# Scores on 64x128 tiles, a widened scale that is transposed, one of two value products scaled by GpSimd, and new step orders in an attention and squared-ReLU kernel

## The chip, the cores and the metric

The kernel runs on one core of a Trainium2 chip. Its time is the device time of one execution in microseconds (us); before the change the median of three runs is 1318.46 us (1316.78 to 1321.82). Five engines work beside each other and wait for each other through semaphores: PE (matrix products and transposes; PEld are its weight loads), DVE (VectorE), ACT (ScalarE), POOL (GpSimd) and SP, which only issues transfers. PE writes to PSUM alone; GpSimd doesn't read PSUM. PSUM has eight banks of 512 float32 columns.

## The reference

Threshold attention over 8 batches, 8 heads, 576 positions and 64 channels, then a two-layer network with a squared ReLU on the 4608 x 512 result. The two weight matrices come as float64.

```python
scores = scale * np.matmul(q, k.transpose(0, 1, 3, 2))
thresh = np.max(scores, axis=-1, keepdims=True) - tau
scores = np.where(scores >= thresh, scores, -1000000000.0)
scores = scores - np.max(scores, axis=-1, keepdims=True)
attn = np.exp(scores)
attn = attn / (np.sum(attn, axis=-1, keepdims=True) + 1e-09)
attn_out = np.matmul(attn, v).astype(np.float32)
...
h = np.maximum(x @ w_in, 0.0)
return (h * h @ w_out).astype(np.float32)
```

## The kernel before

It has an attention stage (to about 519 us) and then the two layers, each as nine steps of 49 products of a twice nested seven-product scheme (L812 and L947). The sums of weight blocks that this scheme needs are made by GpSimd in the attention stage (L122 and L125, 128x512 each).

**Attention, by periods.** The 32 pairs of heads are cut into 144 units of 128 queries (two heads, j = 0 and 1); every ninth unit is made of the 64 rows left over from two pairs. A period takes two units, A and B. `period(p)` walks through a list of step names, written out by hand, and each step records its instructions at that place; so the list fixes the order on every engine's queue. The list CONVERTING serves the periods 2 to 34, in which also one block of float64 weights is turned to float32 (steps c1 to c6, by integer work on ACT, DVE and GpSimd); the list PLAIN serves the others. In plain periods from 35 on, s1 and s2 each issue one GpSimd sum of weight blocks (s2 up to period 59).

**The steps.** `SA` and `SB` are the scores of A and B on PE (L434): 64x64 array tiles, four at once (two heads by two halves of the queries), 512 keys and then the 64 that are left. `SA` holds the leftover keys of both units. `topA0` and the like (L452, DVE) copy a unit's scores from PSUM and take the row maximum; `least` (L459, GpSimd, two columns) adds the threshold; `pow` (L462, ACT) is the exponential; `mask` (L467, DVE, both inputs in SBUF) zeroes what is under the threshold and sums each row. `over` (L474, GpSimd) and `inv` (L477, DVE) make one over the sum. `V`, `W` and `U` turn the weights of finished units on PE (L379, half transposes of 64 rows, so 64*128 tiles), and `eV`, `eW`, `eU` (L523, ACT) bring the result to SBUF as wT. `W` also spreads one over the sum along columns: eight matmuls with the identity (L515, 64*64 tiles). `PV` (L532, 64*64 tiles) is the value product of the units of two periods ago, and `x` (L638, DVE) multiplies its two halves with the spread scales and issues the store of x and the load of new values. `T` and `eT` turn queries and keys of later pairs (L397 on PE; L402 and L410 on ACT) and issue the loads of further ones. `fetch` loads a weight block.

**PSUM.** Scores of A lie in banks 0, 1, 4 and 5, those of B in 1 to 4. `PV` reuses banks 0 and 5, so the next `SA` waits for `x`; `T` uses banks 1 and 4, `W` banks 2 and 3. `U` and `V` share one buffer in banks 6 and 7. The function `touch` adds the waits between instructions of different engines on one bank, which is why the first top waits for the last instruction of `SA`.

**Rings.** Raw weight blocks have four buffers, wT and x two each, values three.

Of the kernel before, what the change touches and what calls it, by code (L numbers as in the profile page):

```python
# [10 lines left out]
FP32 = mybir.dt.float32  # L11
I32 = mybir.dt.int32
U32 = mybir.dt.uint32
ALU = mybir.AluOpType
# [34 lines left out]
def kernel(  # L49
# [25 lines left out]
    nc = tc.nc  # L75
    B, H, S, D = q.shape
    P = 128
# [3 lines left out]
    FULL = S // P  # L81
# [115 lines left out]
    def pick(t, k):  # L197
        return t.rearrange("p (n two) -> p n two", two=2)[:, :, k]

    def convert1(m):  # L200
        if m not in raws:
            return
        lo, hi = pick(raws[m], 0), pick(raws[m], 1)
        a = cv.tile([P, WC], I32, tag="a", bufs=3, name="a")
        nc.scalar.activation(out=a.bitcast(FP32), in_=hi.bitcast(FP32), func=AF.Abs)
        parts[m] = (lo, hi, a)
        raws.pop(m)

    def convert2(m):
        if m in parts:  # L210
            lo = parts[m][0]
            nc.scalar.activation(out=lo, in_=lo.bitcast(U32), func=AF.Copy, bias=0.0, scale=2.0**-29)

    def convert3(m):
# [24 lines left out]
    def convert6(m):  # L239
        if m not in parts:  # L240
            return
        lo, hi, a = parts.pop(m)
        if m < 16:
            a = weight(m)[:, :].bitcast(I32)
        nc.gpsimd.tensor_tensor(out=a, in0=hi, in1=lo, op=ALU.add)
        if m >= 16:
            nc.sync.dma_start(out=slot_of(*chunks[m][1:3]), in_=a.bitcast(FP32))
# [142 lines left out]
    def turn(i, which, spots, other=None):  # L390

        nat, to = loaded.pop((i, which)), places(i)
        of = [nat[:, t, :] for t in range(FULL)] + ([loaded.pop((i, 2))] if which else [])
        for t, x in enumerate(of):
            for r, (spot, at) in enumerate(spots):
                rows = ds(r * HALF, HALF)
                made = nc.tensor.transpose(spot[:, ts(t, HALF)], x[rows, :], ident[rows, rows])  # L397
                touch("turns", made, at, BANK)
        half = FULL * HALF

        def scaled(to, spot):
            touch("turned", nc.scalar.activation(out=to, in_=spot[0], func=AF.Identity, scale=qscale[:, :]), spot[1], BANK, i)  # L402

        def then():
            part = lambda r, x, n: (spots[r][0][:, ds(x, n)], spots[r][1])
            if which:
                for r, n in ((0, half), (1, half + REST)):
                    spot = part(r, 0, n)
                    copy_by = other if r and other else nc.scalar.copy
                    touch("turned", copy_by(to[1][:, ds(r * half, n)], spot[0]), spot[1], BANK, i)  # L410
                scaled(to[2], part(0, half, REST))
                next_keys(i)
            else:
                for r in range(2):
                    scaled(to[0][:, ds(r * half, half)], part(r, 0, half))
                if i + 1 < len(pairs):
                    load_q(i + 1)

        return then
# [3 lines left out]
    def scores(n, rest):  # L423

        of, t = units[n]
        at_k, count = (MAIN, REST) if rest else (0, MAIN)
        for j in range(2):
            first = n % 2 != j
            to = (3 * j + 1) * BANK + first * (BANK - REST) if rest else (3 * j + 2 * first) * BANK
            for c in range(2):  # L430
                rows, at = ds(j * D, D), ds(c * HALF, HALF)
                qT, kT, qR = turned[of[c]]
                lhs = qT[rows, ds((c * FULL + t) * HALF, HALF)] if t < FULL else qR[rows, :]
                made = nc.tensor.matmul(  # L434
                    sc[at, ds(to, count)], lhs, kT[rows, ds(at_k, count)], start=True, stop=True
                )
                touch("scores", made, to, count, of[c])

    def softmax(n):

# [40 lines left out]
    def do(n, what, *args):  # L481
        if n in soft:
            soft[n][what](*args)

    wT = {}
# [13 lines left out]
    def fill(m, f, pt, at=None):  # L499

        first, count = FILLS[f]
        if m not in wT:
            wT[m] = sb.tile([P, (2 * CH + 2) * P], FP32, tag="wT", bufs=W_RING, name="wT")
        for i, (u, c) in enumerate(FIRST[first : first + count]):
            half_turn(pt, i, weights[2 * m + u][:, c, :, :].rearrange("p j d -> p (j d)"), at)
        if f == "W":
            rs = smalls.pop(m)
            for j in range(2):
                for r in range(2):
                    rows = ds(r * HALF, HALF)  # L510
                    for u in range(2):
                        one = rs[rows, 3, 2 * u + j : 2 * u + j + 1]
                        wide = bass.AP(tensor=one.tensor, offset=one.offset, ap=[one.ap[0], [0, D]])
                        to = pt[ds(u * D, D), r, ts(count + j, HALF)]
                        made = nc.tensor.matmul(to, wide, ident[rows, rows], start=True, stop=True)  # L515
                        touch("turns", made, at and at + r * BANK, BANK)

    def filled(m, f, pt, at=None):

# [69 lines left out]
    def begun(n):  # L589
        return starts.get(n)  # L590

    PLAIN = """
        SA c3 T topA0 over U eU s1 SB topA1 powA1 leastA topB0 powB0 c1 s2 PV c4 V fetch
        inv powA0 c5 topB1 powB1 eT maskA1 x W eV maskA0 leastB c2 c6 eW maskB0 maskB1
    """.split()
    CONVERTING = """
        fetch c3 SA c1 SB topA1 over s1 U topA0 c2 powA1 topB0 topB1 eU leastA maskA1
        leastB inv powA0 PV powB0 W maskA0 x powB1 maskB0 T c4 c5 maskB1 eT V c6 eW eV
    """.split()

    def spots():
# [5 lines left out]
    def period(p):  # L607
# [26 lines left out]
        def given_out():  # L634
            if has(2 * m):
                x = sb.tile([P, 2, P], FP32, tag="x", bufs=2, name="x")
                for j in range(2):
                    made = nc.vector.tensor_tensor(  # L638
                        out=x[:, j, :], in0=sc[:, ds(5 * j * BANK, P)], in1=wT[m][:, ts(SCALE_AT + j, P)], op=ALU.mult
                    )  # L640
                    touch("x", made, 5 * j * BANK, P, m)
                wT.pop(m)
                valued(m)
                give_x(m, x)
            ask(False)

# [12 lines left out]
        def every(key):  # L659
# [8 lines left out]
            "PV": PV, "x": given_out,  # L668
# [4 lines left out]
        }  # L673
        steps["over"] = lambda: do(a, "over")
        steps["inv"] = lambda: do(a, "inverse")
        for letter, n in (("A", A), ("B", B_)):
# [533 lines left out]
```

## Time and profile before

| what | us |
|---|---|
| median of three runs | 1318.46 |
| the runs | 1321.82, 1318.46, 1316.78 |
| span of the profiled execution, first to last instruction | 1314.0 |
| PE busy, share | 1277.6, 97% |
| DVE busy, share | 1016.3, 77% |
| ACT busy, share | 849.6, 65% |
| POOL busy, share | 839.0, 64% |
| last tops of the attention stage end near | 508 |
| first product of the layers | 519.4 |

The granted clock of TensorE is 0.998 over the span. What a run's time holds beyond the span lies around the first and the last instruction. In a group of the profile one reads line, engine, operation, destination and source, shapes and count, then the busy time in us, the mean of one in ns, and the engine's idle time ahead of the group with what ended it. In a timeline one reads start and length in us, engine, line and operation.

### The profile page before, as it was taken

To read this page: it belongs to the slowest core of one execution; us is meant where nothing else is said; L and a number is where in the kernel's file an instruction comes from. 1 tells how busy PE (TensorE), PEld (TensorE's weight loads), DVE (VectorE), ACT (ScalarE), POOL (GpSimd) and SP (SyncE) were. 2 spreads that over 40 slices of the span, in tenths; PEclk is the share of its full clock that TensorE was granted. 3 is DMA by queue.
4 is the path that set the end of the run, shared out by engine and by line. 5 is a ranking of instruction groups with operands and counts; after the bars stand their busy time and mean duration, and the time that the engine had idled before them with its cause. 6 is when DMAs were issued, how large, how long until landed. Compare 5 with 4: busy or idle time off the path is not lost.

```text
span 1314.0 us, 47792 instructions
## 1 busy us (share of the span) xinstructions
PE 1277.6 (97%) x19483; PEld 1141.4 (87%) x19483; DVE 1016.3 (77%) x2497; ACT 849.6 (65%) x1464; POOL 839.0 (64%) x958
## 2 busy tenths in 40 slices
PE   7999999899999999999999999999999999999998
PEld 5666666677777777999999999999999999999998
DVE  5999999999999996877887788777656654665463
ACT  5999999888989886566756675665524322432240
POOL 1444444455555421778987888758777777777775
PEclk9999999999999999999999999999999999999999
DMA  5555566544433322466656655669645135423411
GB/s 135 143 160 142 155 174 182 149 103 99 101 78 86 77 60 46 148 206 192 195 180 210 197 187 179 193 232 394 249 161 161 48 115 162 161 63 100 161 33 33
DMA packets 247035, 192.12 MB, mean 146 GB/s; under 512 B 97184, under 2 KB 195488, under 8 KB 246816
## 3 DMA queue, kind: packets, MB, share of 16 engines
q1 hardware_dynamic: 245360, 188.63, 47.4%
q8 instruction: 153, 2.51, 0.8%
q10 hardware_dynamic: 1456, 0.44, 0.1%
q14 instruction: 66, 0.54, 0.1%
HBM read 116.65 MB, written 72.35 MB: 144 GB/s over the span
## 4 chain that ended last, share of the span: by engine, by line
PE 85%; ACT 8%; DVE 3%; issue 2%; DMA 1%; SPq 1%; POOL 0%; ACTq 0%; DVEq 0%; POOLq 0%
PE ph L812 30%; PE po L947 28%; PE sc L434 9%; PE sc L532 8%; PE pt L379 5%; ACT arena L523 3%; ACT arena L462 3%; PE sc L397 2%; PE sc L515 2%; DVE arena L452 1%; PE sc L379 1%; DMA wall<-w 1%; ACT arena L402 1%; DVE arena L467 0%; DMA arena<-in_k_dram 0%
## 5 line engine op out<-in xcount | busy, mean ns | idle before, releaser
L125 POOL TENSOR_TENSOR arena<-arena 128x512 f32<-128x512 f32 (+1 forms) x314 | 378.0, 1222 | 134.5 <-DVE arena L125 120.5
L947 PE MATMUL po<-wall,arena 128*128 128x128 f32 x3528 | 395.0, 275 | 1.6 <-ACT arena L724 1.4
L947 PEld LDWEIGHTS po<-wall,arena 128*128 128x128 f32 x3528 | 394.3, 192 | 2.2 <-ACT arena L724 1.8
L812 PE MATMUL ph<-arena,wall 128*128 128x128 f32 x3528 | 394.2, 275 | 0.7 <-DVE arena L638 0.7
L812 PEld LDWEIGHTS ph<-arena,wall 128*128 128x128 f32 x3528 | 394.0, 192 | 0.8 <-issue 0.8
L125 DVE TENSOR_TENSOR arena<-ph,arena 128x512 f32<-128x512 f32 x378 | 256.4, 689 | 86.2 <-PE ph L812 66.0
L122 POOL TENSOR_TENSOR arena<-arena 128x128 f32<-128x128 f32 (+2 forms) x314 | 255.2, 814 | 48.6 <-DMA arena<-w 31.9
L125 DVE TENSOR_TENSOR arena<-po,arena 128x128 f32<-128x128 f32 x378 | 108.4, 290 | 167.6 <-PE po L947 163.4
L467 DVE SCALAR_TENSOR_TENSOR arena<-arena 128x576 f32<-128x576 f32 x288 | 229.6, 817 | 2.7 <-ACT arena L462 1.7
L462 ACT ACTIVATE arena<-arena 128x576 f32<-128x576 f32 x288 | 208.2, 778 | 14.1 <-DVE arena L452 7.0
L452 DVE TENSOR_SCALAR_CACHE_REDUCE arena<-sc 128x576 f32<-128x576 f32 x288 | 205.5, 751 | 13.3 <-ACT arena L523 5.5
L758 ACT COPY c<-arena 128x512 f32<-128x512 f32 (+1 forms) x303 | 173.5, 579 | 50.4 <-DVE arena L122 41.3
L532 PEld LDWEIGHTS sc<-arena 64*64 64x64 f32 x5760 | 154.0, 133 | 55.3 <-DVE arena L452 28.7
L532 PE MATMUL sc<-arena 64*64 64x128 f32 (+1 forms) x5760 | 176.7, 263 | 18.1 <-DVE arena L452 11.6
L122 DVE TENSOR_TENSOR arena<-arena,c 128x512 f32<-128x512 f32 (+1 forms) x267 | 174.9, 663 | 6.1 <-ACT c L758 4.0
L434 PE MATMUL sc<-arena 64*64 64x64 f32 (+1 forms) x2304 | 167.4, 414 | 5.6 <-ACT arena L402 5.6
L523 ACT COPY arena<-pt 128x1024 f32<-128x1024 f32 x144 | 146.6, 1018 | 24.8 <-PE pt L379 24.4
L724 ACT COPY arena<-po 128x128 f32<-128x128 f32 x63 | 16.6, 264 | 186.4 <-PE po L947 183.7
L459 POOL TENSOR_SCALAR arena<-arena,tau_p 128x2 f32<-128x2 f32 x144 | 75.1, 521 | 73.4 <-DVE arena L452 67.8
L724 ACT COPY arena<-ph 128x512 f32<-128x512 f32 x63 | 36.6, 581 | 124.2 <-PE ph L812 123.5
L379 PEld LDWEIGHTS pt<-ident,arena 64*128 64x128 f32 x2304 | 83.1, 139 | 38.2 <-ACT arena L523 25.6
L434 PEld LDWEIGHTS sc<-arena 64*64 64x64 f32 x2304 | 59.2, 134 | 52.2 <-ACT arena L402 26.4
(46 smaller groups left out, 896.1 us busy)
## 6 DMA issues: line engine op xcount, KB each, us to landing
g<-arena SPq DMA_DIRECT2D x144, 256.0 KB, 2.4
arena<-g SPq DMA_DIRECT2D x144, 256.0 KB, 4.4
w<-arena SPq DMA_DIRECT2D x60, 256.0 KB, 2.4
wall<-w SPq DMA_DIRECT2D x49, 256.0 KB, 5.2
arena<-w SPq DMA_DIRECT2D x44, 256.0 KB, 3.2
arena<-in_v_dram SPq DMA_DIRECT2D x32, 288.0 KB, 3.6
out_dram<-arena SPq DMA_DIRECT2D x70, 128.0 KB, 2.2
arena<-in_q_dram SPq DMA_DIRECT2D x64, 128.0 KB, 3.2
```

The costliest lines, as they stand in the source:

```text
L122: e.tensor_tensor(out=out, in0=x, in1=y, op=ALU.subtract)
L125: e.tensor_tensor(out=out, in0=x, in1=y, op=ALU.add)
L379: made = nc.tensor.transpose(pt[:, r, ts(slot, HALF)], of[rows, :], ident[rows, rows])
L434: made = nc.tensor.matmul(sc[at, ds(to, count)], lhs, kT[rows, ds(at_k, count)], start=True, stop=True)
L452: made = nc.vector.tensor_scalar(out=s[:, j, :], in0=sc[:, ds(at, S)], scalar1=1.0, scalar2=None, op0=ALU.mult, op1=ALU.min, accum_out=nmx ...
L462: nc.scalar.activation(out=w[:, :, j, :], in_=of(j), func=AF.Exp, bias=nmx[:, j : j + 1], scale=-1.0)
L467: nc.vector.scalar_tensor_tensor(out=w[:, :, j, :], in0=of(j), scalar=thr[:, j : j + 1], in1=w[:, :, j, :], op0=ALU.is_le, op1=ALU.mult, a ...
L523: touch("weights", nc.scalar.copy(joined(to), whole(pt, 0, count)), at, 2 * BANK, m)
L532: made = nc.tensor.matmul(sc[ds(u * D, D), ds(5 * j * BANK + row, count)], loaded_v[i][rows, (c - (u != j)) % CH, :], wT[m][rows, ds(weigh ...
L758: nc.scalar.copy(c, y)
L812: nc.tensor.matmul(to[:, j, :], W_IN[m, k][:, ts(j, P)], of[k][:, m - 1, :], start=(not more and j == 0), stop=True, skip_group_check=True,)
L947: nc.tensor.matmul(to, g[:, j, :], w[:, j, :], start=(not more and j == 0), stop=(j == 3), skip_group_check=True)
```

## The change

Five things are done.

1. The scores are made on 64x128 tiles: for a unit of one pair, one matmul per head over all 128 queries in place of two over 64. For that the transposed queries are stored in natural order. The leftover units keep 64x64 tiles.
2. One over the sum is spread by GpSimd: the step `spread` (function `widen`) copies the four columns to 128x256 in the part of wT that `W` will overwrite, and `W` turns this copy with four half transposes in place of the eight matmuls of L515.
3. Of the two halves of the value product, DVE scales the first as before; the second is copied from PSUM by ACT, and the new step `xs` multiplies it by its scales on GpSimd. `xs` also issues the stores.
4. Both lists of steps get a new order. In PLAIN, s2 now stands ahead of `over`, and `U` ahead of `SA`; in CONVERTING, `T` opens the period.
5. c2 may now run ahead of c1.

```diff
     def convert2(m):
-        if m in parts:
-            lo = parts[m][0]
+        if m in raws or m in parts:
+            lo = pick(raws[m], 0) if m in raws else parts[m][0]
...
             else:
+                blocks = to[0].rearrange("p (t r q) -> p r t q", r=2, q=HALF)
                 for r in range(2):
-                    scaled(to[0][:, ds(r * half, half)], part(r, 0, half))
+                    spot, at = part(r, 0, half)
+                    scaled(blocks[:, r, :, :], (spot.rearrange("p (t q) -> p t q", q=HALF), at))
...
-            for c in range(2):
-                rows, at = ds(j * D, D), ds(c * HALF, HALF)
-                qT, kT, qR = turned[of[c]]
-                lhs = qT[rows, ds((c * FULL + t) * HALF, HALF)] if t < FULL else qR[rows, :]
-                made = nc.tensor.matmul(
-                    sc[at, ds(to, count)], lhs, kT[rows, ds(at_k, count)], start=True, stop=True
-                )
-                touch("scores", made, to, count, of[c])
+            rows = ds(j * D, D)
+            if t < FULL:
+                qT, kT, _ = turned[of[0]]
+                parts = [(ds(0, P), qT[rows, ts(t, P)], kT, of[0])]
+            else:
+                parts = [(ds(c * HALF, HALF), turned[i][2][rows, :], turned[i][1], i) for c, i in enumerate(of)]
+            for at, lhs, kT, i in parts:
+                made = nc.tensor.matmul(sc[at, ds(to, count)], lhs, kT[rows, ds(at_k, count)], start=True, stop=True)
+                touch("scores", made, to, count, i)
...
         if f == "W":
-            rs = smalls.pop(m)
             for j in range(2):
-                for r in range(2):
-                    rows = ds(r * HALF, HALF)
-                    for u in range(2):
-                        one = rs[rows, 3, 2 * u + j : 2 * u + j + 1]
-                        wide = bass.AP(tensor=one.tensor, offset=one.offset, ap=[one.ap[0], [0, D]])
-                        to = pt[ds(u * D, D), r, ts(count + j, HALF)]
-                        made = nc.tensor.matmul(to, wide, ident[rows, rows], start=True, stop=True)
-                        touch("turns", made, at and at + r * BANK, BANK)
+                half_turn(pt, count + j, wT[m][:, ts(SCALE_AT + j, P)], at)
+
+    def widen(m):
+
+        if m not in wT:
+            wT[m] = sb.tile([P, (2 * CH + 2) * P], FP32, tag="wT", bufs=W_RING, name="wT")
+        one = smalls.pop(m)[:, 3, 0:1]
+        wide = bass.AP(tensor=one.tensor, offset=one.offset, ap=[one.ap[0], [1, 2], [2, 2], [0, D]])
+        to = wT[m][:, ds(SCALE_AT * P, 2 * P)].rearrange("p (j u d) -> p j u d", j=2, u=2)
+        nc.gpsimd.tensor_copy(out=to, in_=wide)
...
     PLAIN = """
-        SA c3 T topA0 over U eU s1 SB topA1 powA1 leastA topB0 powB0 c1 s2 PV c4 V fetch
-        inv powA0 c5 topB1 powB1 eT maskA1 x W eV maskA0 leastB c2 c6 eW maskB0 maskB1
+        fetch U s2 SA over SB topA0 eU topA1 powA0 leastA s1 topB0 V inv topB1 spread powA1 maskA1 eV powB0 leastB powB1 PV T maskA0 W x maskB1 eT maskB0 eW xs
     """.split()
     CONVERTING = """
-        fetch c3 SA c1 SB topA1 over s1 U topA0 c2 powA1 topB0 topB1 eU leastA maskA1
-        leastB inv powA0 PV powB0 W maskA0 x powB1 maskB0 T c4 c5 maskB1 eT V c6 eW eV
+        fetch T SA c3 topA1 SB over c2 U topA0 eU topB1 topB0 c4 inv powA1 powA0 leastA PV leastB powB0 eT maskA1 x maskA0 powB1 V maskB0 spread W c5 eW c6 eV xs maskB1 c1
     """.split()
...
+                by_vector = (0,)
                 for j in range(2):
-                    made = nc.vector.tensor_tensor(
-                        out=x[:, j, :], in0=sc[:, ds(5 * j * BANK, P)], in1=wT[m][:, ts(SCALE_AT + j, P)], op=ALU.mult
-                    )
+                    by = sc[:, ds(5 * j * BANK, P)], wT[m][:, ts(SCALE_AT + j, P)]
+                    if j in by_vector:
+                        made = nc.vector.tensor_tensor(out=x[:, j, :], in0=by[0], in1=by[1], op=ALU.mult)
+                    else:
+                        made = nc.scalar.copy(x[:, j, :], by[0])
                     touch("x", made, 5 * j * BANK, P, m)
+                late["x"] = x, [j for j in range(2) if j not in by_vector], wT[m]
                 wT.pop(m)
                 valued(m)
+
+        def scaled_x():
+            if has(2 * m):
+                x, js, by = late["x"]
...
+                for j in js if len(js) == 1 else ():
+                    nc.gpsimd.tensor_tensor(out=x[:, j, :], in0=x[:, j, :], in1=by[:, ts(SCALE_AT + j, P)], op=ALU.mult)
                 give_x(m, x)
             ask(False)
```

By queue, in a plain period of the changed kernel: PE has U, SA, SB, V, PV, T, W; DVE topA0, topA1, topB0, inv, topB1, maskA1, maskA0, x, maskB1, maskB0; ACT eU, powA0, powA1, eV, powB0, powB1, the copy of x, eT, eW; GpSimd s2, over, leastA, s1, spread, leastB, xs. In a converting period: PE has T, SA, SB, U, PV, V, W; DVE topA1, topA0, topB1, topB0, c4, inv, maskA1, x, maskA0, maskB0, c5, maskB1; ACT c2, eU, powA1, powA0, powB0, eT, the copy of x, powB1, eW, eV, c1; GpSimd c3, over, leastA, leastB, spread, c6, xs.

More of the change, by code (lines that the diff above doesn't have):

```diff
@@ L206, in convert1 @@
         parts[m] = (lo, hi, a)
-        raws.pop(m)
     def convert2(m):
-        if m in parts:
-            lo = parts[m][0]
+        if m in raws or m in parts:
+            lo = pick(raws[m], 0) if m in raws else parts[m][0]
             nc.scalar.activation(out=lo, in_=lo.bitcast(U32), func=AF.Copy, bias=0.0, scale=2.0**-29)
@@ L242, in convert6 @@
         lo, hi, a = parts.pop(m)
+        raws.pop(m)
         if m < 16:
@@ L636, in given_out @@
                 x = sb.tile([P, 2, P], FP32, tag="x", bufs=2, name="x")
+                by_vector = (0,)
                 for j in range(2):
-                    made = nc.vector.tensor_tensor(
-                        out=x[:, j, :], in0=sc[:, ds(5 * j * BANK, P)], in1=wT[m][:, ts(SCALE_AT + j, P)], op=ALU.mult
-                    )
+                    by = sc[:, ds(5 * j * BANK, P)], wT[m][:, ts(SCALE_AT + j, P)]
[3 more added lines that the diff above has]
+                        made = nc.scalar.copy(x[:, j, :], by[0])
                     touch("x", made, 5 * j * BANK, P, m)
+                late["x"] = x, [j for j in range(2) if j not in by_vector], wT[m]
                 wT.pop(m)
                 valued(m)
+        def scaled_x():
+            if has(2 * m):
+                x, js, by = late["x"]
+                if len(js) == 2:
+                    nc.gpsimd.tensor_tensor(
+                        out=x[:, :, :].rearrange("p j q -> p (j q)"), in0=x[:, :, :].rearrange("p j q -> p (j q)"),
+                        in1=by[:, ds(SCALE_AT * P, 2 * P)], op=ALU.mult,
+                    )
+                for j in js if len(js) == 1 else ():
+                    nc.gpsimd.tensor_tensor(out=x[:, j, :], in0=x[:, j, :], in1=by[:, ts(SCALE_AT + j, P)], op=ALU.mult)
                 give_x(m, x)
@@ L667, in period @@
             "SA": scored_a, "SB": scored_b,
-            "PV": PV, "x": given_out,
+            "PV": PV, "x": given_out, "xs": scaled_x,
             "c1": lambda: convert1(begun(p)), "c2": lambda: convert2(begun(p)),
@@ L673, in period @@
         }
+        steps["spread"] = lambda: has(2 * m + 2) and widen(m + 1)
         steps["over"] = lambda: do(a, "over")
```

## The prediction

> **What bounds the kernel now.** I read the table of windows first, to find the stages. Its columns are PE, PEld, DVE, ACT and POOL busy, then clock, DMA share, GB/s.
>
> ```profile
> 100.00:150.00 50.00, 46.34 (x1164) 31.83 (x1158) 49.37 (x144) 47.43 (x77) 22.08 (x33) 1.00 0.53 141
> ...
> 400.00:450.00 50.00, 49.35 (x1322) 37.35 (x1320) 47.99 (x145) 44.62 (x70) 25.73 (x37) 1.00 0.37 86
> ...
> 700.00:900.00 200.00, 200.00 (x1794) 200.00 (x1793) 155.48 (x244) 127.16 (x229) 154.76 (x179) 1.00 0.63 211
> ```
>
> Everything the change touches lies before 519 us. The two layers behind it keep PE busy without a gap and are untouched: 0 for them. In the converting periods (first row) DVE is busy 98.7%, ACT 95%. In the plain ones (second row) PE is the fullest and DVE has 96%. So no engine alone is the answer in the plain ones.
>
> From the timeline I took the start of every fourth L452 as the start of a period. The 33 converting periods (24.3 to 268.2 us) take 7.39 us on average, the quick ones 7.19. The 25 plain periods with two GpSimd sums each (to 433.4 us) take 6.61, the quick ones 6.44; eight with one sum 6.58; three with none 6.43.
>
> Then the groups, for durations (mean ns of one after the comma), here by form:
>
> ```profile
> L638 DVE TENSOR_TENSOR arena<-sc,arena 128x128 f32<-128x128 f32 x120 | 29.1, 285 | 0.2
> ...
> L219 POOL TENSOR_SCALAR arena<-arena 128x512 f32<-128x512 f32 x28 | 17.1, 611 | 0.0
> ...
> L474 POOL TENSOR_SCALAR arena<-arena 128x4 f32<-128x4 f32 x61 | 14.1, 232 | 85.7 <-DVE arena L467 83.3
> ...
> L122 POOL TENSOR_TENSOR arena<-arena 128x384 f32<-128x384 f32 x4 | 4.0, 1002 | 0.2
> ```
>
> What an instruction costs its engine is the distance to the next start, which the timeline gives: L452 (top) 0.68, L467 (mask) 0.74, L638 0.20, reciprocal 0.09, L227 0.46, L235 0.61 on DVE; L462 (power) 0.67, an eviction of 1024 columns 0.90, of 512 0.47 on ACT.
>
> PE, one plain period:
>
> ```profile
> 408.28 2.22 PEld L532 LDWEIGHTS sc<-arena 64*64 64x64 f32 x71 [0.28 <-issue]
> ...
> 410.67 0.57 PEld L379 LDWEIGHTS pt<-ident,arena 64*128 64x128 f32 x16 [0.17 <-issue]
> ...
> 411.16 0.20 PEld L379 LDWEIGHTS sc<-ident,arena 64*128 64x128 f32 x4
> ...
> 411.43 0.32 PEld L515 LDWEIGHTS sc<-ident,arena 64*64 64x64 f32 x16
> ```
>
> Each row is one step; 64*64 and 64*128 are the array tiles. Between neighbours with unlike tiles there is a hole: 0.17 us between the value product and the transposes, 0.07 before L515. By single starts, a change of tile costs 0.10 us, and the first pass behind it 0.05 more: 0.15. Four such changes stand in a plain period.
>
> Last the waits of GpSimd and masks on each other, from two timelines:
>
> ```profile
> 270.96 1.28 POOL L122 TENSOR_TENSOR wall<-wall 128x512 f32<-128x512 f32 x1
> 272.21 0.79 POOL L459 TENSOR_SCALAR arena<-arena,tau_p 128x2 f32<-128x2 f32 x1
> ```
>
> and, on DVE:
>
> ```profile
> 271.63 1.22 DVE L467 SCALAR_TENSOR_TENSOR arena<-arena 128x576 f32<-128x576 f32 x1
> 272.78 0.08 DVE L467 DVE_READ_ACCUMULATOR arena<-arena 128x1 f32 x1
> ```
>
> A mask (two inputs from SBUF) that finds a GpSimd sum running takes 1.22 instead of 0.81 us: it starts in earnest 0.19 us before the sum's end. The small L459 that waits behind this mask takes 0.79 instead of 0.29: it starts 0.68 after the mask did. The tops (one input from PSUM) and the sums don't disturb each other. So masks and GpSimd exclude each other.
>
> **The change, part by part.**
>
> 1. *Scores on 64x128 tiles.* Half the matmuls per period (16 fewer loads and 16 fewer passes), but the same streams: four quadrants ran at once, 0.431 us per 512-column pass, and two wide tiles need the same passes. Gain by themselves 0. The new order stands them next to transposes of the same tile, so two of four changes of tile go: 0.30 us. No row shows a wide matmul that isn't a transpose. Bounds: 0, if the two tiles run side by side as the half transposes do (a pair per 0.062 us); +0.43 per 512-column score step, if the second tile waits for the first one's second pass. I take 0: the quadrants do overtake each other so. The Trainium skill (TensorE: Matmul & The Clock Gate, LDWEIGHTS) has a load last by its columns, about 107 ns for 128 against 53 for 64; by it the 64-column passes would grow by an estimated 0.05 each, 0.2 a period. The trace disagrees: loads of 128 columns show 139 ns against 133, and pairs follow each other at 0.062.
> 2. *Spread.* 16 passes of L515 (four groups at 0.058 = 0.23 us) go, four transposes (two pairs, 0.12) come. PE's plain period: 6.16 us of work with the changes of tile, then 5.75.
> 3. *Widening copy on GpSimd, 128x256.* No row shows one. Between 0.23 (four columns, L474) and 0.61 (512 columns, L219); half way by columns 0.42.
> 4. *One of two L638.* DVE loses 0.20. ACT gets a copy of 128x128; the page has L724 with 0.264, its slot about 0.16. GpSimd gets a 128x128 product: 384 columns take 1.00, 512 take 1.28, so 0.45 (bounds 0.23 and 1.00).
> 5. *Orders.* DMA issues move with their steps on SP: the store of x now waits for GpSimd. x has two buffers and a landing takes 2 to 4 us, so this stays hidden; if it didn't, the next x would wait.
>
> *Converting periods.* DVE then has 4x0.68 + 0.46 + 0.09 + 4x0.74 + 0.20 + 0.61 = 7.03. ACT had 6.6 to 6.7 and gets 0.16; PE 5.75. On GpSimd, the copy comes when the first mask ends, 0.68 after its start; the vector product of 0.20 stands between that mask and the next, and covers the copy up to 0.45. The conversion's last add (L245, 1.2) waits for the last mask and runs under the tops. In the slower old periods the mask behind the reciprocal waited 0.10 to 0.16 for its power; in the new order each power ends before its mask's turn. So 7.03, with 0.05 for the periods with a rest unit: 7.08 against 7.39, times 33 = **-10.2 us**.
>
> *Plain periods with sums.* I lay one out from the first top, t = 0. DVE alone would need 6.16 - 0.20 = 5.96. Loop over ACT: powers at 0.80 and 1.48, eviction 2.15, powers 3.05 and 3.73, copy of x 4.40, done 4.66; then scores 1.09 and 0.25 to the next top: 6.0. PE: top at 1.5, 2.27 for values with the change of tile and release, T, W and U 1.05, scores 1.34: 6.1. All three have room under what GpSimd does to the masks. The first small step (L459) starts at 1.56, the sum behind it 1.82 to 3.10: mask 1 at 2.91 instead of 2.78. The copy runs 3.58 to 4.00: mask 2 at 3.81. The second L459 4.48 to 4.77: mask 3 at 4.83. The product comes when mask 3 ends, 5.50 to 5.95: mask 4 at 5.76, the end 6.50. With 0.07 for rest units 6.57 against 6.61: 25 x -0.04 = **-1.0**. One sum: the same, 8 x -0.01 = -0.1. No sum: only the product hurts, 6.20 against 6.43, **-0.7**. What DVE and PE are relieved of is given back to GpSimd.
>
> Sum -12.0. The profiled execution spans 1314.0 and would span 1302; the median of the runs is 1318.46, 4.5 above that span. Forecast **1306**, own range 1298 to 1313.
>
> **Rivals.**
>
> *A sum between two masks (slower).* The other sum of a period no longer waits for the last mask through L474: it stands right behind the product. In my layout the copy of x is done at 4.66, GpSimd can begin the product near 4.76, and mask 3 asks at 4.83. If the product is first, mask 3 moves to 5.02; the sum, waiting, gets its turn at 5.70, before mask 4 asks at 5.76; mask 4 then starts at 5.70 + 1.28 - 0.19 = 6.79, and the period is 7.53. That is 25 x 0.92 = +23, less 11 for the rest: **1330**. The order is decided by 0.07 us, less than I know the copy (it decides from 0.35 up), ACT's copy or a semaphore's way. For it: the central numbers. Against it: it needs both that the product wins, and that a waiting GpSimd instruction beats the next mask, which the trace shows only with a reciprocal between; and two further waits (for the store of the old x) stand ahead of the product on GpSimd's queue, where an instruction with a wait elsewhere starts 0.09 behind the one before it. The Trainium skill (SBUF — State Buffer, Who interferes with whom) says that the one that issues first holds the shared port for its whole instruction and the other fully blocks; that favours this rival, and the 1.22 us mask bears it out but for the last 0.19.
>
> *GpSimd starves.* If DVE keeps masks back to back, the copy waits for mask 2 and ends at 4.62; W, U and the scores follow, next top 6.77. 33 plain periods get 0.17 worse, +6 - 11: **1313**. No row shows it.
>
> *Wide tiles one after the other.* PE 5.75 + 0.86 = 6.6 in plain periods, hidden in the converting ones: +3 - 11, **1311**. Against it: the overtaking quadrants.
>
> **How the numbers follow.** Forecast 0.55 (0.50 of it faster by over 0.5%, which is 6.6 us and about what a measurement of this kernel tells from no change); the sum between masks 0.30, slower; the two others 0.15, of which 0.05 faster and 0.10 within. The range has to reach the slow rival: 1297 to 1332. Faster 0.55, same 0.15, slower 0.30.
>
> **What would show it.** Converting periods at 7.0 to 7.1 with L515 gone and holes on PE only around the value product. Plain periods at 6.5 with masks of 0.9 to 1.1 us; if one mask in four takes 1.8 us in the plain periods with two sums, the rival holds. Score steps of over 1.2 us per 512 columns prove the wide tiles wrong. Scale transposes waiting for GpSimd would show starving. The prediction is wrong if converting periods stay above 7.3: then DVE wasn't their bound.

## The result: slower, by a sum between two masks

The changed kernel takes **1334.69 us** (median of 4 runs, 1333.93 to 1334.93) against 1318.66 before on the same chip (4 runs, 1316.78 to 1321.82): ratio 1.0119, 95% interval 1.0102 to 1.0137. The forecast was 1306; the rival "a sum between two masks" had said 1330. The profiled execution spans 1333.1 us, at a mean clock of 0.996 (before: 1314.0 at 0.998), 19.1 us more. The medians differ by 16.0. Most executions on record take 1.8 us more than their span; so by my estimate the profiled execution of before took some 1315.8, less than any of the four timed ones, and some 3 us of the 19.1 come from that.

The table of windows of the changed kernel; columns PE, PEld, DVE, ACT and POOL busy, then clock, DMA share, GB/s:

```profile
100.00:150.00 50.00, 46.37 (x1012) 35.15 (x1010) 49.60 (x143) 49.72 (x88) 31.27 (x51) 1.00 0.56 143
400.00:450.00 50.00, 45.92 (x976) 33.73 (x972) 50.00 (x121) 39.89 (x69) 37.04 (x48) 1.00 0.31 69
```

In the plain periods (second row) PE fell from 49.35 to 45.92 and ACT from 44.62 to 39.89, while POOL rose from 25.73 to 37.04 and DVE shows no idle time at all, in a kernel in which DVE was given less to do. It is held, not at work. The masks of the whole profile, in its table of groups:

```profile
L470 DVE SCALAR_TENSOR_TENSOR arena<-arena 128x576 f32<-128x576 f32 x288 | 264.7, 947 | 2.2 <-POOL arena L520 0.6
```

And before:

```profile
L467 DVE SCALAR_TENSOR_TENSOR arena<-arena 128x576 f32<-128x576 f32 x288 | 229.6, 817 | 2.7 <-ACT arena L462 1.7
```

The mean grew by 130 ns, and 288 times 130 ns is 37 us of DVE. 24 masks of over 1.2 us, one in each of the periods 35 to 58, hold 24 of them. The timeline of one plain period, from mask 3 to the next top, DVE's masks and GpSimd's work (start, length):

```profile
398.93 0.46 POOL L660 TENSOR_TENSOR arena<-arena 128x128 f32<-128x128 f32 x1
398.95 1.05 DVE L470 SCALAR_TENSOR_TENSOR arena<-arena 128x576 f32<-128x576 f32 x1
...
399.35 1.79 POOL L125 TENSOR_TENSOR wall<-wall 128x512 f32<-128x512 f32 x1
...
399.93 1.81 DVE L470 SCALAR_TENSOR_TENSOR arena<-arena 128x576 f32<-128x576 f32 x1
```

Read it in the order of asking. The product (L660) starts 0.02 us ahead of mask 3 (16 to 28 ns by the single starts of all 24 such periods), so mask 3 waits for it and shows 1.05 in place of 0.81. The sum behind the product stands recorded from 399.35 but shows 1.79 for 1.28 of work: it waits until mask 3 has had its turn. Mask 4 starts at 399.93, when the sum is already waiting, and shows 1.81: it waits for the whole sum.

**Where the 19 us come from.** Starts of every fourth top, as in the prediction. Means per period in us; "periods 0 to 2" and "34 and 35" are sums of three and of two periods:

| kernel | periods 0 to 2 | converting, 3 to 33 | 34 and 35 | two sums, 36 to 59 | one sum | none |
|---|---|---|---|---|---|---|
| before | 21.43 | 7.38 | 14.54 | 6.585 | 6.58 | 6.43 |
| changed | 24.74 | 7.14 | 18.08 | 7.418 | 6.55 | 6.28 |

That is +3.3, 31 x -0.238 = -7.4, +3.5, 24 x 0.833 = **+20.0**, 8 x -0.04 = -0.3 and 3 x -0.16 = -0.5: 18.7. The stretch from there to the layers takes 0.8 less, the first loads 0.1 less. The layers take 1.4 more; they are untouched, and in the single profiles of all the kernels here they take 794.4 to 797.7 us.

The two joints, between the start and the converting periods and between these and the plain ones, were in no term of mine. The waits at the second one are in the changed kernel's timeline:

```profile
263.73 0.96 PE L379 MATMUL pt<-ident,arena 64*128 64x64 f32 x16 [2.48 <-ACT arena L527]
...
267.27 0.76 DVE L455 TENSOR_SCALAR_CACHE_REDUCE arena<-sc 128x576 f32<-128x576 f32 x1 [3.65 <-PE sc L439]
```

PLAIN now begins with `U`, which shares its PSUM buffer with `V`; in the first plain period it waits for the eviction that stands last but three in CONVERTING, with the scores queued behind it on PE. DVE then waits 3.65 us for those.

### The profile page after: what moved, and what is told of

It is laid out like the page before. It is cut to its first block, busy times and chain, and to the rows that moved or that the text cites. A ratio compares the mean times of both kernels' runs of the same rounds, so it can differ in the third digit from the quotient of the medians.

```text
span 1333.1 us, 44245 instructions
## 1 busy us (share of the span) xinstructions
PE 1280.2 (96%) x17595; PEld 1160.7 (87%) x17595; DVE 1034.2 (78%) x2425; ACT 852.7 (64%) x1536; POOL 934.9 (70%) x1102
## 5 line engine op out<-in xcount | busy, mean ns | idle before, releaser
L470 DVE SCALAR_TENSOR_TENSOR arena<-arena 128x576 f32<-128x576 f32 x288 | 264.7, 947 | 2.2 <-POOL arena L520 0.6
L455 DVE TENSOR_SCALAR_CACHE_REDUCE arena<-sc 128x576 f32<-128x576 f32 x288 | 202.3, 748 | 15.0 <-PE sc L439 7.7
L536 PE MATMUL sc<-arena 64*64 64x128 f32 (+1 forms) x5760 | 173.6, 262 | 15.0 <-DVE arena L455 10.9
L439 PE MATMUL sc<-arena 64*128 64x64 f32 (+3 forms) x1280 | 181.4, 444 | 3.4 <-ACT arena L402 3.1
L536 PEld LDWEIGHTS sc<-arena 64*64 64x64 f32 x5760 | 150.7, 133 | 30.4 <-DVE arena L455 27.9
L379 PEld LDWEIGHTS pt<-ident,arena 64*128 64x128 f32 x2304 | 89.3, 139 | 58.9 <-ACT arena L527 29.0
L439 PEld LDWEIGHTS sc<-arena 64*128 64x128 f32 (+1 forms) x1280 | 86.4, 180 | 42.9 <-issue 25.4
L462 POOL TENSOR_SCALAR arena<-arena,tau_p 128x2 f32<-128x2 f32 x144 | 64.8, 450 | 81.8 <-DVE arena L455 77.8
L379 PE MATMUL pt<-ident,arena 64*128 64x64 f32 x2304 | 103.3, 225 | 9.9 <-DVE arena L470 5.7
```

The costliest lines, as they stand in the source:

```text
L379: made = nc.tensor.transpose(pt[:, r, ts(slot, HALF)], of[rows, :], ident[rows, rows])
L439: made = nc.tensor.matmul(sc[at, ds(to, count)], lhs, kT[rows, ds(at_k, count)], start=True, stop=True)
L455: made = nc.vector.tensor_scalar(out=s[:, j, :], in0=sc[:, ds(at, S)], scalar1=1.0, scalar2=None, op0=ALU.mult, op1=ALU.min, accum_out=nmx ...
L470: nc.vector.scalar_tensor_tensor(out=w[:, :, j, :], in0=of(j), scalar=thr[:, j : j + 1], in1=w[:, :, j, :], op0=ALU.is_le, op1=ALU.mult, a ...
L536: made = nc.tensor.matmul(sc[ds(u * D, D), ds(5 * j * BANK + row, count)], loaded_v[i][rows, (c - (u != j)) % CH, :], wT[m][rows, ds(weigh ...
```

## The experiments

The theory, A: masks and GpSimd exclude each other, the one that asks first goes first, and s2 ahead of `over` lets a sum get in between masks 3 and 4. The rivals: the place of the sum is harmless and something else in the order, the wide tiles, the split of x or the spread by transposes costs the time. All times are medians, ratios are to the kernel before on the same chip (1318.04, 1318.05 and 1319.47 in the three groups). The table holds all kernels by stage, as above, from one profile each; mask 4 is the mean of the last mask in the periods 35 to 59. The converting column is to be read with care: in several profiles one to three converting periods are much longer than the rest (in e6 8.89, 8.29 and 7.71), so that e5 and e6, with the same steps and the same list there, differ by 0.12.

| kernel | 0 to 2 | conv. | 34, 35 | two | one | none | mask 4 | time | ratio, interval |
|---|---|---|---|---|---|---|---|---|---|
| e1_over_first | 23.95 | 7.13 | 16.84 | 6.650 | 6.54 | 6.28 | 0.82 | 1315.08 | 0.9973, 0.9961 to 0.9986 |
| e2_both_by_vector | 24.36 | 7.15 | 16.46 | 7.190 | 6.51 | 6.23 | 0.81 | 1329.11 | one run |
| e3_split_sum | 25.77 | 7.15 | 17.14 | 6.981 | 6.55 | 6.28 | 1.32 | 1327.67 | one run |
| e4_over_first_narrow | 23.94 | 7.13 | 17.18 | 6.621 | 6.46 | 6.27 | 0.82 | 1316.01 | 0.9982, 0.9969 to 0.9995 |
| e5_joints | 21.87 | 7.11 | 15.78 | 6.647 | 6.50 | 6.28 | 0.82 | 1313.61 | 0.9966, 0.9954 to 0.9978 |
| e6_old_plain_order | 21.70 | 7.23 | 14.86 | 7.014 | 7.11 | 6.39 | 0.97 | 1325.35 | 1.0055, 1.0040 to 1.0069 |
| e7_both_by_vector | 21.93 | 7.15 | 15.24 | 6.594 | 6.50 | 6.24 | 0.81 | 1311.55 | 0.9953, 0.9934 to 0.9971 |
| e8_old_spread | 22.12 | 7.21 | 16.18 | 6.738 | 6.79 | 6.40 | 0.99 | 1321.72 | 1.0029, 1.0017 to 1.0041 |
| e9_two_pieces | 24.54 | 7.11 | 15.91 | 6.981 | 6.95 | 6.75 | 1.00 | 1331.47 | 1.0089, 1.0072 to 1.0107 |
| e9b_four_pieces | 26.27 | 7.11 | 16.05 | 7.100 | 7.08 | 6.79 | 1.04 | 1333.49 | 1.0112, 1.0095 to 1.0128 |
| e10_best | 22.82 | 7.23 | 14.61 | 6.596 | 6.52 | 6.23 | 0.81 | 1310.27 | 0.9937, 0.9925 to 0.9950 |
| e11_old_converting | 22.05 | 7.41 | 17.84 | 6.647 | 6.50 | 6.28 | 0.82 | 1322.76 | 1.0025, 1.0013 to 1.0037 |

**e1: the second sum behind `over` again.**

```diff
-        fetch U s2 SA over SB topA0 ...
+        fetch U SA over s2 SB topA0 ...
```

> The changed kernel with one step moved in PLAIN: s2 behind over, so that the second sum again waits for the period's last mask. Theory A (the ungated sum gets between mask 3 and mask 4): no mask over 1.1 us is left, the 25 plain periods with two sums go from 7.47 to about 6.5 us, the time to 1334.7 - 25 x 0.97 = about 1310. Rival B (the product on GpSimd is what holds the masks up, the sum is only near it): mask 3 still finds the product in front, the period stays at 7.4, the time near 1335. Rival C (the wide score tiles or the new order on PE cost it): no change either, 1335.

1315.08: some 19 us come off by one word's place, and periods with two sums fall from 7.418 to 6.650. Its timeline, the same part of a period:

```profile
346.29 0.45 POOL L660 TENSOR_TENSOR arena<-arena 128x128 f32<-128x128 f32 x1
346.35 1.00 DVE L470 SCALAR_TENSOR_TENSOR arena<-arena 128x576 f32<-128x576 f32 x1
...
347.29 0.81 DVE L470 SCALAR_TENSOR_TENSOR arena<-arena 128x576 f32<-128x576 f32 x1
...
348.19 0.23 POOL L477 TENSOR_SCALAR arena<-arena 128x4 f32<-128x4 f32 x1 [1.46 <-DVE arena L470]
...
348.50 1.27 POOL L125 TENSOR_TENSOR wall<-wall 128x512 f32<-128x512 f32 x1
```

The product still goes ahead of mask 3. But the next thing in GpSimd's queue is `over` (L477), which waits for mask 4, so that mask 4 takes 0.81 and the sum runs under the tops. The time is 5 us over what A expected, because a period comes to 6.65 and not to 6.5: masks 1 to 3 keep their waits (means 1.04, 0.94 and 1.01). The two joints stay as well (23.95 and 16.84), as A's sum had assumed.

**e2: both halves of the product on DVE, the order as changed.**

```diff
-                by_vector = (0,)
+                by_vector = (0, 1)
```

> The changed kernel with both halves of the value product scaled on DVE again (no copy on ACT, no product on GpSimd), the order of steps as changed. Theory A: the sum now stands right behind the small threshold step, which mask 3 waits for; so it is first and mask 3 takes 1.8 us in place of mask 4; period 7.2 to 7.5, time 1328 to 1336. Rival B: without the product the periods fall to 6.5, time near 1310. Rival C: 1335.

1329.11. With the product gone nothing stands ahead of the sum any more, and it takes its turn one mask earlier:

```profile
395.66 1.26 POOL L125 TENSOR_TENSOR wall<-wall 128x512 f32<-128x512 f32 x1
...
395.86 1.68 DVE L470 SCALAR_TENSOR_TENSOR arena<-arena 128x576 f32<-128x576 f32 x1
```

Mask 3 pays now. So the product isn't the cause; the sum without a gate is.

**e3: the sum in two halves of 256 columns, the second behind `over`.**

```diff
+            cuts = (0, BANK // 2, BANK) if split[0] else (0, BANK)
+            for c, d in zip(cuts, cuts[1:]):
+                split[1] = d < BANK
+                yield op(nc.gpsimd, to[:, c:d], x[:, c:d], y[:, c:d])
```

> The changed kernel with the ungated weight sum cut in two by columns: the first 256 columns where it stood, the other 256 behind over. The work is the same. Theory A: the wait of mask 4 follows the length of what runs in front of it, 0.73 in place of 1.28 us for the GpSimd instruction; mask 4 takes 1.25 instead of 1.81, the 22 periods concerned 6.9 instead of 7.47; time 1334.7 - 22 x 0.55 = about 1323. If the loss were one of the number of GpSimd instructions (a fixed handover each), the time would rise above 1335; by rival C it stays.

In the 21 periods in which the sum is cut, mask 4 falls from 1.81 to 1.27, by 0.54, and the period from 7.47 to 6.92. In the last three the sum is still whole, and mask 4 takes 1.81; the means of the table mix the two. A half sum that nothing blocks takes 0.72, so 0.56 less than a whole one. The wait goes with the length of the sum, as A says. The time, 1327.67 in a single run, is 5 us over what I expected. In the profile 4 of these lie outside the cut periods: the first top comes 1.65 us later than in the changed kernel, the first three periods take 1.0 more, and the stretch to the layers 1.3 more.

**e4: e1 with scores on 64x64 tiles and the old storage of the queries** (the diff's first part undone).

> The first kernel of this call (s2 behind over) with the scores on 64x64 tiles again and the transposed queries stored as before. It prices the wide tiles alone. Theory A: PE has 0.3 us of room in a period, so the tiles and the changes of tile that they save are worth 0 to 0.15 us in plain periods and nothing in converting ones: 0 to +6 us over the first kernel. Rival C: narrow tiles make it faster by over 5 us.

1316.01 against 1315.08, intervals of the ratios overlapping: the wide tiles are worth nothing that these runs can tell. By stages the narrow ones are even 0.01 to 0.08 us better in plain periods; why is told below, under wide tiles.

**e5: e1 with an own list for periods 0, 1 and 35**, the old PLAIN order with the new steps in it:

```diff
+    JOINT = """
+        SA T topA0 over U eU s1 SB topA1 powA1 leastA topB0 powB0 s2 PV V fetch
+        inv powA0 topB1 spread powB1 eT maskA1 x W eV maskA0 leastB eW maskB0 maskB1 xs
+    """.split()
```

> The second sum behind the step over, as in e1_over_first, and besides an own list JOINT for the periods 0, 1 and 35: the old PLAIN order (T behind SA, U behind the first top, c steps left out), with spread between inv's tops and W, and xs at the end. If the first two periods are long because T stands late in the new PLAIN, and period 34 because U stands ahead of SA in period 35 and waits there for the last eviction of a converting period, then periods 0 and 1 together fall from 15.9 to about 14, period 34 from 9.6 to about 7.2, and the time to 1310 to 1312 (e1: 1315.1). The rival: both only move a wait for data that are late anyway (first loads, last conversion); then the next periods get longer by as much and the time stays within 1.5 us of 1315.

The start gives back 2.1 us (23.95 to 21.87). Period 34 falls as expected, to 6.98, but period 35 grows to 8.80, so that the pair gains only 1.1. The two together gain 3.1 us in the trace. The time, 1313.61, lies within the rival's 1.5 us of 1315, and the intervals of e1 and e5 overlap: that the time gains by this list isn't shown, and at the second joint half of the wait was only moved on, as the rival had it.

**e6: that list in all plain periods.**

```diff
-        for name in CONVERTING if converts(p) else JOINT if p in (0, 1, max(starts) + 2) else PLAIN:
+        for name in CONVERTING if converts(p) else JOINT:
```

> The list JOINT for every period that doesn't convert: the old PLAIN order with the new steps, the new CONVERTING order. s2 stands ahead of PV, so that both sums run under the tops and in front of the first mask, and none can come between two masks. If only the place of the second sum among the masks made the kernel slow, periods with two sums take 6.6 to 6.8 and the time is 1310 to 1318, whatever else is new in the order of PLAIN. If the new PLAIN order is worth what two changes of tile less are (0.30 us in 36 periods), it is 8 to 11 us above e5_joints.

1325.35, above the first expectation (1310 to 1318) and just over the second one's upper end: 11.7 us over e5. From period 36 on no mask takes over 1.11, yet periods with two sums take 7.01 and those with one 7.11. In the latter PE has no idle time (40.00 of 40.00 us in the window from 440 to 480). The old order suited the old steps; for the new ones the new order is worth 0.37 to 0.6 us a period.

**e7: e5 with both halves of the product on DVE.**

> e5_joints with both halves of the value product on DVE: DVE gets 0.20 us per period, ACT loses 0.15, GpSimd 0.46. If, as the prediction has it, what DVE is relieved of is given back to GpSimd through blocked masks, plain periods come out within 0.1 us of e5_joints and only the converting ones are longer, by 0.03 to 0.2: 0 to +6 us on e5_joints. If the split is worth its full 0.20 in all periods, +14 us.

1311.55, 2.1 us under e5 where 0 to 6 over it were expected, with overlapping intervals. The split is worth nothing that these runs can tell: without it periods with two sums are 0.05 shorter, converting ones 0.04 longer. Why the 0.20 us don't show in the converting ones is in the windows from 60 to 255 us, of the changed kernel:

```profile
60.00:255.00 195.00, 179.91 (x4006) 137.73 (x4000) 191.88 (x547) 192.97 (x337) 118.61 (x191) 1.00 0.63 166
```

and of e7:

```profile
60.00:255.00 195.00, 174.85 (x4021) 135.21 (x4012) 194.11 (x574) 189.45 (x310) 105.92 (x164) 1.00 0.63 165
```

With the split ACT is busy 99% (192.97 of 195); without it DVE is (194.11), with ACT at 97%. By single periods, the quickest with the split are at 6.87, DVE's work without a gap, but most are at 7.03 to 7.3; without it 13 of 31 are at 7.06 to 7.08, which is 6.87 + 0.20, and nearly all others at 7.10 to 7.29. The split lowers DVE's floor by 0.20 us, but it gives ACT the copy, and by its share ACT then has no room left to let DVE reach that floor. This is read from the shares; no run took work off ACT alone.

**e8: e5 with the eight matmuls with the identity in the place of `spread`.**

> e5_joints with the eight matmuls with the identity in the place of the GpSimd copy and its four half transposes. PE gets some 0.11 of passes and two changes of tile (0.30), 0.4 us per period, and GpSimd loses a copy of 0.39 that a mask waits for. If masks and GpSimd, which exclude each other, bound the plain periods, these get shorter by 0.1 to 0.3 in spite of PE: 4 to 10 us under e5_joints, the converting ones the same. If PE is the bound in plain periods, they get longer by up to 0.4: up to 14 us over it.

1321.72, 8.1 us over e5: the rival's side. Its window (first) and e5's (second) over periods with one sum:

```profile
440.00:480.00 40.00, 40.00 (x938) 31.20 (x938) 37.49 (x107) 35.62 (x63) 18.76 (x29) 1.00 0.41 97
```

```profile
440.00:480.00 40.00, 39.39 (x911) 30.95 (x906) 39.07 (x111) 36.84 (x65) 21.27 (x37) 1.00 0.35 79
```

PE has no idle time in e8, and DVE is idle for 2.5 us. So spreading by GpSimd is worth 0.29 us where one sum runs, and 0.09 where two do and the masks take it back. These and the periods without a sum make 4.9 of the 8.1 us. In the converting periods the two kernels agree but for a few, of which two of e8 take 7.91 and 8.62; whether these belong to the spread isn't shown.

**e9 and e9b: the changed kernel, with ACT's copy in two or four pieces**, so that the product asks later; no step is moved.

```diff
-                        made = nc.scalar.copy(x[:, j, :], by[0])
+                        n = 1 if converts(p) else 2
+                        for c in range(n):
+                            made = nc.scalar.copy(x[:, j, ts(c, P // n)], sc[:, ds(5 * j * BANK + c * P // n, P // n)])
```

> The changed kernel with nothing moved; only ACT's copy of the second product half is made in two pieces of 64 columns in all periods that don't convert, so that GpSimd's product can ask for its turn a little later, by some 0.1 us (an estimate from the 0.15 us that the whole copy takes of ACT). In the changed kernel the product is 16 ns ahead of mask 3. If the order of asking decides, mask 3 is now first, the product comes behind it, mask 4 asks while the product holds and so is ahead of the second sum: mask 4 takes 1.0 to 1.1 instead of 1.78 us, periods with two sums 6.6 to 6.8, the time is 1314 to 1320. In quicker periods the distance may come out otherwise, and 0.1 us may be too little; then some periods are of the one kind and some of the other. If the second sum takes its turn ahead of mask 4 whoever asks first, mask 4 stays at 1.8 and the time at 1334.

> The same with four pieces of 32 columns, which puts the product off by 0.25 to 0.4 us. By the order of asking mask 4 falls to 1.0 to 1.1 in every period with two sums; the next scores wait for the copy, so that periods of 6.7 to 7.0 are expected and 1316 to 1324. By the other reading 1.8 and 1334 or more.

The mechanism comes out as A has it, the time doesn't. The timeline of e9:

```profile
348.02 0.82 DVE L470 SCALAR_TENSOR_TENSOR arena<-arena 128x576 f32<-128x576 f32 x1
...
348.60 0.55 POOL L662 TENSOR_TENSOR arena<-arena 128x128 f32<-128x128 f32 x1 [0.62 <-ACT arena L647]
...
348.76 1.00 DVE L470 SCALAR_TENSOR_TENSOR arena<-arena 128x576 f32<-128x576 f32 x1
...
349.11 1.78 POOL L125 TENSOR_TENSOR wall<-wall 128x512 f32<-128x512 f32 x1
...
350.09 0.76 DVE L455 TENSOR_SCALAR_CACHE_REDUCE arena<-sc 128x576 f32<-128x576 f32 x1 [0.31 <-ACT arena L527]
```

Mask 3 is ahead and takes 0.82. Mask 4 asks at 348.76 while the product holds, goes right behind it (1.00), and now it is the sum that waits: recorded from 349.11 with 1.78, it still has most of its 1.28 to do when the top starts at 350.09. The order of asking decides. (One instruction of each engine waits at a time; so these runs can't tell this rule from one by which the two engines take turns.) But the pieces cost more than 0.1 us: the first starts 0.53 later in its period than the whole copy had (4.92 against 4.39 from the first top), 0.15 behind the end of DVE's half in place of beside it. In the code, `touch`, which also takes away waits between instructions on different banks, is called for the last piece only; that the first piece so keeps a wait for DVE fits the 0.15, but no run tried it the other way. Scores and evictions behind it come later too, and the plain periods without a second sum, which have nothing to gain, grow by 0.4 to 0.5. With four pieces it is the same: mask 4 takes 1.04, the period 7.10 and not 6.7 to 7.0, and the time is 1333.49.

**e10: e7 with another list for period 35**, the new order with `U` behind SB.

```diff
+    BETWEEN = """
+        fetch SA over s2 SB topA0 U eU topA1 powA0 leastA s1 topB0 V inv ...
```

> e7_both_by_vector with another list for period 35 alone: the new PLAIN order with the second sum behind over and U behind SB, so that the scores of period 35 wait neither for the last eviction of period 34 nor, as in JOINT, a mask for two sums. The four periods 33 to 36 take 28.82 us there; 27.3 to 28.0 expected, and 1 us less in all: 1310 to 1311. If the wait is only moved on, 1311.5 to 1312.

1310.27, ratio 0.9937: **faster than both kernels**. Periods 34 and 35 are at 14.61, as before the change (14.54). The four periods 33 to 36 take 28.28, a little above the 27.3 to 28.0 expected. Its profiled execution has two converting periods of 8.75 and 8.38, and that of e6 two of 8.89 and 8.29. In both, the transposes `T` wait for a load of queries (1.4 us in e10, 1.0 in e6), and behind it DVE stands still three times, for 1.6, 0.4 and 0.7 us in e10, which is nearly all that these two periods are longer. Why the load is late in some executions stays open. That it beats e7 isn't shown, since the intervals overlap.

**e11: e5 with the old CONVERTING order.**

> e5_joints with the old CONVERTING order (spread put behind inv, xs ahead of eV). DVE has the same work, 7.01 us by its starts. If the old order costs what the prediction says, waits of a mask for its power of 0.10 to 0.16, converting periods are at 7.2 to 7.3 instead of 7.14: 2 to 5 us above e5_joints. If the order of CONVERTING was what made the converting periods shorter, and not the relief of DVE, they are back at 7.39: 8 us above it.

1322.76, by the two ratios 7.8 us over e5: converting periods are back at 7.41, where they were before the change (7.38), with all the new steps in them. In 12 of the 31 periods its second mask takes 0.95 to 1.05 us, because the spread goes ahead of it:

```profile
133.01 1.04 DVE L470 SCALAR_TENSOR_TENSOR arena<-arena 128x576 f32<-128x576 f32 x1
133.05 0.40 POOL L520 COPY arena<-arena 128x256 f32<-128x256 f32 x1
```

The copy takes 0.40, not the 0.93 of a blocked one, though the mask is recorded 0.04 us ahead of it. These 12 masks make less than a third of the 0.30 us. For the rest, the window from 60 to 255 us shows DVE and ACT with more idle time than in the changed kernel (188.10 and 186.62 in place of 191.88 and 192.97):

```profile
60.00:255.00 195.00, 171.15 (x3806) 128.12 (x3804) 188.10 (x525) 186.62 (x324) 117.08 (x183) 1.00 0.62 162
```

DVE's tops wait there for scores on PE for 3.3 us in all, against 1.8 in the changed kernel. The new order is what made the converting periods shorter; which of its moves did it was not tried.

## Why the prediction was wrong, point by point

- **The step that failed** is the wait of mask 4 in the plain periods with two sums. The forecast's layout let the product come when mask 3 ends (5.50 to 5.95), had mask 4 wait for the product alone, and put a wait for the second sum at nothing; that wait stood in a rival with 0.30. The runs show the product ahead of mask 3 and the sum ahead of mask 4, which takes 1.81 us: 24 x 0.833 = 20.0 us. e1, which gates the sum again, is some 19 us faster.
- **Why that step went wrong.** My layout had the copy of x done at 4.66, the product asking near 4.76 and mask 3 at 4.83; the trace has 4.64, 4.72 and 4.74, counted from the first top. The central numbers said that the product is first and that 1330 follows. What I put against it, two further waits on GpSimd's queue, costs nothing there. That a waiting GpSimd instruction beats the next mask I held for doubtful; the 1.81 us mask shows it, and e9 shows the reverse with the order reversed. The Trainium skill (SBUF — State Buffer, Who interferes with whom) has whoever issues first hold the shared port; these runs agree, 1.81 against 1.00 us for the same mask.
- **The rival's sizes** held: mask 4 at 1.8, the period at 7.53 against 7.42, 25 x 0.92 = 23 us against 20.0. That its total of 1330 came so near 1334.69 is in part luck: it had 3 us too many for the sum, nearly 3 too many taken off in the converting periods, and nothing for the joints.
- **Converting periods**: 7.08 forecast, 7.14 measured, but the reason was wrong. I ascribed the gain to DVE's 0.20 us; undone alone it costs 0.04 (e7), and the order alone 0.30 (e11). DVE's floor was near (7.03, the terms of which add up to 7.04; the quickest periods take 6.87). ACT, which I put at 6.6 to 6.7 and 0.16 more, is busy 99% there.
- **Plain periods without the sum between the masks**: 6.57 forecast, 6.65 in e1. "What DVE and PE are relieved of is given back to GpSimd" holds: e1's masks take 1.07, 0.94, 1.00 and 0.81, 0.5 us more than the four before, and DVE is busy for 129.07 of 130 us there. I had counted waits of masks 1, 2 and 4, of 0.13, 0.16 and 0.19; it is mask 3 that waits for the product, in mask 4's place. What makes the 0.08 us that are left isn't shown.
- **One sum, none**: 6.55 and 6.28 measured, with -0.3 and -0.5 us beside my -0.1 and -0.7.
- **Missed terms**: the joints, +3.3 at the start and +3.5 at periods 34 and 35. Each list was laid out against itself alone. And the 4.5 us that I took from the span to the median were too many: it is 1.8 in most executions, the rest is that the profiled one was quick. The layers I had put at 0 because PE has no gap there; PE is busy for 198.35 us of the 200 from 900 to 1100 us, so they have small ones, and they came out 1.4 us longer.
- **Wide tiles**: gain 0, right, and the two do run side by side: two matmuls start 7 ns apart. But the reason had a mistake. I let the loads of transposes (139 ns) decide, and loads of 128 columns of queries take longer:

```profile
L439 PEld LDWEIGHTS sc<-arena 64*128 64x128 f32 x1024 | 79.6, 192 | 35.6 <-issue 20.9 <-ACT arena L402 7.8 <-ACT arena L645 2.1
L439 PEld LDWEIGHTS sc<-arena 64*64 64x64 f32 x256 | 6.9, 137 | 7.7 <-issue 4.4 <-ACT arena L402 2.5
```

  These groups are of e1, wide and narrow side by side: 192 against 137 ns. The Trainium skill (TensorE: Matmul & The Clock Gate, LDWEIGHTS) has about 107 against 53: other lengths, the same distance. By single starts, pairs of 64-column passes stand mostly 0.11 us apart in e1, where the groups of four in e4 stand 0.06 apart, and 512-column passes 0.48 to 0.53 against 0.43 to 0.48. So the 0.05 us that the prediction set aside are there. They cost next to no time, as e4 shows; the 0.08 us between e1 and e4 in periods with one sum have this sign.
- **GpSimd's new work**: the spread takes 0.40 where nothing blocks it (e11; I took 0.42), the product 0.46 (0.45).
- **GpSimd starves** and **wide tiles one after the other** didn't happen: the copy ends at 3.94 from the first top, not at 4.62, and wide pairs go side by side.

## What to carry to other kernels

When instructions of two engines exclude each other, lay out the order in which they ask, for each instruction that no wait holds back; a long one that could stand waiting got its turn here between two short ones, and the gate that kept it out cost nothing. Where central numbers and a feeling differ, forecast by the numbers. Price a new order of steps also where one list follows another, and test each part alone: here the order of the converting periods carried the gain, the plain order and the spread were each worth 5 to 12 us only beside the other new steps (plain periods with two sums take 6.59 in e7 and took 6.585 before), two parts were worth nothing, and one word's place cost some 19 us.

## What was not expected of the hardware

- A few hundredths of a us between two starts decide over 0.8 us, in 24 periods running, each of 7.46 to 7.48 us: the order locks itself in. The recorded start is not quite the moment that counts: a mask recorded 0.04 us ahead of a GpSimd instruction still lost (e11), one 0.10 ahead won (masks of 0.80 against a product, in the periods 59, 61, 63 and 65 of the changed kernel).
- Loads of 64x128 tiles take 192 ns with queries as weights and 139 with transposes.
- The first top comes 10.5 to 13.7 us into the span, 13.7 in e5 and 10.9 in e6, which have the same list there. Spans of single profiles are therefore compared from the first top on.
